# Gated linear attention with a two-way maxout layer: another order of the first loads, another split of one weight difference, and other costs in the planner

## The chip, the cores and the metric

The kernel runs on one core of one Trainium2 chip. The metric is the device time of one execution in microseconds (us); lower is better. One core has TensorE (PE in the profile, its weight loads PEld), VectorE (DVE), ScalarE (ACT), GpSimd (POOL) and SyncE (SP), which here issues every DMA.

## The reference

Inputs are q, k, v and alpha of shape (4, 8, 768, 48): 4 batch elements, 8 heads, 768 tokens, 48 values per head. For each batch element and head a 48x48 state runs over the tokens, and its output rows become the tokens of a two-way maxout layer with weights w1, w2 (384x1024) and w_out (1024x384). The output is (3072, 384) in float32.

```python
for t in range(S):
    state = alpha[:, :, t, :, None] * state + np.einsum('bhd,bhe->bhde', k[:, :, t], v[:, :, t])
    y[:, :, t] = np.einsum('bhd,bhde->bhe', q[:, :, t], state)
x = np.ascontiguousarray(y.transpose(0, 2, 1, 3)).reshape(B * S, H * D)
out = np.maximum(x @ w1, x @ w2) @ w_out
```

## The kernel before

**The attention half.** The 768 tokens of the first batch element are taken as three "doubles" of 256 tokens (written (0, h), (1, h), (2, h), with h = 0, 1 for the two halves of the heads); the other 2304 tokens as 18 "singles" of 128 tokens, numbered 6 to 23. Each goes through the same steps: the logarithm of alpha on ACT (`a1`); sums over the tokens on PE (`p1`, tile dcs or cs); the two exponentials `en` and `ep` and the small `gg` on ACT; k times `en` on POOL (`kt`); q times `ep` on DVE (`qt`); eight transposes on PE (`p2`, tile dtp or tp) and one copy of them (`v2`, tile dqk or qk, on ACT or DVE); the products of q and k on PE (`p3`, tiles dpa and dpb, in a ring of two PSUM buffers); two masked copies of these on DVE (`m0`, `m1`, tile dpt or pt); the state's update (`pk` or `kv` on PE, `w` on DVE, tile dw, and `g`, `t32`, `T0`, `T1` on POOL); the output y on PE (`p4`, tile dy or y); and its copy into xT on ACT (`a3`).

**The maxout half.** Since max(a, b) = b + relu(a - b), the kernel forms wd = w1 - w2 (`prep_wd`, tile wd16: six pieces of 128x512, four on DVE and two on POOL) and m = w2 @ w_out (`w2c` converts w2, `w2t` transposes it on PE, `w2te` copies the transposes, `m` multiplies by the converted w_out `wo16`, `mev` copies the result). The tokens that are in xT are taken in groups of one to three blocks of 128. For each group there are eight steps `f` (three matmuls h = wd x, then a relu on ACT or DVE into g16), and for each block two steps `t`: half 0 (three matmuls with m, three with w_out) and half 1 (five with w_out). `oev` copies the finished block and `st` stores it. The tiles h, op, mp and y share a ring of three PSUM buffers.

**What sets the order.** A planner, class Sched, runs while the kernel is built. Each step is an Op with a cost per engine, the steps that it depends on (`deps`, which count in the planner's clock), steps that only have to be placed before it (`after`), the buffers that it allocates and reads, and a priority. Whenever an engine is free by the planner's clock, the ready step with the earliest start is placed next in that engine's queue. On the chip each engine runs its queue in that order and waits at a step whose inputs are not there. `refill` forms the groups of the maxout half when PE would have nothing else to do. So a cost that is changed moves nothing by itself, but may change the order of all queues.

**The loads.** SP issues them in one queue: the first double in seven DMAs, w2 in one, w_out in two halves, w1 in two halves (columns 0 to 511 and 512 to 1023), the second and third doubles in four DMAs of 384 KB each (alpha, k, q, v), then the singles, which reuse the memory of the weights. The first four of the eight `f` steps of a group need the first half of wd, the others the second:

```python
            o = op("f", a, {"PE": 3 * max(W / 2400 + 0.0025, 0.07)}, lambda e, a0=a0, W=W, f=f: fstep(a0, W, f),
                   lat=0.17, deps=xs + wdc[f // NFH], after=pend[-1:], alloc=[bh] + ([bg] if f == 0 else []), prio=1000 + a)
```

Of the kernel before, what the change touches and what calls it, by code (L numbers as in the profile page):

```python
# [49 lines left out]
class Sched:  # L50
# [49 lines left out]
    def run(self):  # L100
        while True:
            c = self.pick("PE")
            if c and self.refill:
                self.refill(c[1], c[1] > self.free["PE"] + 0.3)
            best = None
            for e in self.todo:
                c = self.pick(e)
                if c and (best is None or c[1] < best[0]):
                    best = (c[1], e, c[2])
            if best is None:  # L110
                if self.refill and self.refill(1e9, True):
                    continue
                break
            t, e, op = best
            cost = op.engs[e]
            if e == "PE" and op.tiled != self.tiled:
                cost += 0.09
                self.tiled = op.tiled
            if e == "SP":
                t = max(t, self.wire - 4.0)  # L120
                self.wire = max(self.wire, t + 0.7) + cost
                op.done = self.wire + op.lat
                cost = 0.45
            else:
                op.done = t + cost + op.lat
            self.free[e] = t + cost
            for b in op.alloc:
                b.ring.taken.append(b)
            for x in op.engs:
                self.todo[x].remove(op)  # L130
            op.fn(e)
        assert not any(self.todo.values()), {e: [(o.name, o.n) for o in v][:5] for e, v in self.todo.items()}
# [3 lines left out]
def kernel(  # L136
# [21 lines left out]
    nc = tc.nc  # L158
# [485 lines left out]

    def prep_wd(e, s, i):
        c = slice(i * FH, (i + 1) * FH)
        eng = nc.vector if e == "DVE" else nc.gpsimd
        eng.tensor_sub(out=wd16[:, s, c], in0=w1f[:, s, c], in1=w2f[:, s, c])  # L648

# [68 lines left out]
    def op(*a, **k):  # L718
        return Op(S, *a, **k)
# [31 lines left out]

    dloads_of(0, 0.0)
    lw2 = prev = op("w2", 0, {"SP": WLOAD}, lambda e: load_w2(), lat=1.6, after=[prev], prio=0.5)
    lw1, lwo = [], []
    for kind in ("wo", "w1"):
        for i in range(2):
            fn = {"wo": load_wo, "w1": load_w1}[kind]
            prev = op(kind, i, {"SP": WLOAD / 2}, lambda e, i=i, fn=fn: fn(i), lat=1.6, after=[prev], prio=0.5)
            (lwo if kind == "wo" else lw1).append(prev)
    dloads_of(1, 0.3)  # L760
    dloads_of(2, 0.6)

    w2c = [
        op("w2c", s, c, lambda e, s=s: copy(e, w216[:, s, :], w2f[:, s, :]), deps=[lw2], prio=0.6)
        for s, c in enumerate(({"ACT": 0.95}, {"DVE": 0.65}, {"ACT": 0.95, "DVE": 0.65}))
    ]
    wdc = [[op("wd", s, {"POOL": 1.2} if s == 2 else {"DVE": 0.68}, lambda e, s=s, i=i: prep_wd(e, s, i),
               deps=[lw1[i], lw2], prio=0.6) for s in range(3)] for i in range(2)]
    woc = [op("woc", f, {"ACT": 0.75, "DVE": 0.55},
# [26 lines left out]
    sp1 = op("pads", 1, {"DVE": 0.5}, lambda e: set_pads(1), prio=0.9)  # L796
    smask = op("mask", 0, {"DVE": 1.0}, lambda e: set_mask(), prio=0.1)
    sdv = [op("dvT", i, {"POOL": 0.6}, lambda e, i=i: set_dvT(i), prio=(-1, 0.9)[i]) for i in range(2)]
    sone = [op("one", i, {"POOL": 0.8}, lambda e, i=i: set_single(i), prio=1.5) for i in range(4)]


    rdloga, rdqt, rdkt, rdv, rdT, rdw, rdt32, rdgg, rdg = (Ring(2) for _ in range(9))
    B2 = []
    for m in range(ND):
# [11 lines left out]
        def add(name, h, engs, fn, deps, lat=0.1, alloc=(), reads=(), **kw):  # L816
            o = GD[m - 1].get((name, h)) if m else None
            g[name, h] = op("d" + name, (m, h), engs, fn, lat=lat, deps=deps, after=[o, g.get((name, h - 1))],
                            alloc=[B[x] for x in alloc], reads=[B[x] if not isinstance(x, Buf) else x for x in reads],
                            prio=2 * m + 0.3 * h, **kw)  # L820
            return g[name, h]

        for h in range(2):
            al = lambda x: [x] if h == 0 else []
            re = lambda x: [x] if h else []
            add("a1", h, {"ACT": 0.43}, lambda e, m=m, h=h: d1(m, h), [g["ld", 0, h], sp1 if m == 1 else None],
                alloc=al("loga"), reads=[L[0]] + re("loga"))
            add("p1", h, {"PE": 0.5}, lambda e, m=m, h=h: dcs(m, h), [g["a1", h]], lat=0.17, alloc=[("cs", h)], reads=["loga"])
            add("en", h, {"ACT": 0.39}, lambda e, m=m, h=h: dexp(m, h, "en", -1.0), [g["p1", h]],
                alloc=al("en"), reads=[("cs", h)] + re("en"))  # L830
            add("ep", h, {"ACT": 0.39}, lambda e, m=m, h=h: dexp(m, h, "ep", 1.0), [g["en", h]],
                alloc=al("ep"), reads=[("cs", h)] + re("ep"))
            add("gg", h, {"ACT": 0.2}, lambda e, m=m, h=h: dgg(m, h), [g["ep", h]],
                alloc=al("gg"), reads=[("cs", h)] + re("gg"))
            add("kt", h, {"POOL": 1.0}, lambda e, m=m, h=h: dqk(m, h, 1), [g["en", h], g["ld", 1, h]],
                alloc=al("kt"), reads=["en", L[1]] + re("kt"))
            add("qt", h, {"DVE": 0.7}, lambda e, m=m, h=h: dqk(m, h, 2), [g["ep", h], g["ld", 2, h]],
                alloc=al("qt"), reads=["ep", L[2]] + re("qt"))
# [3 lines left out]
                alloc=[("tp", h)], reads=["qt", "kt"])  # L842
            add("v2", h, {"DVE": 0.64, "ACT": 0.92}, lambda e, m=m, h=h: dtpe(e, m, h), [g["p2", h]],
                alloc=[("qk", h)], reads=[("tp", h)])
            add("p3", h, {"PE": 0.36}, lambda e, m=m, h=h: dp(m, h), [g["v2", h]], lat=0.17,
                alloc=[("pa", h), ("pb", h)], reads=[("qk", h)], tiled=True)
            for t in range(2):
                add("m" + str(t), h, {"DVE": 0.62}, lambda e, m=m, h=h, t=t: dmask(m, h, t),
                    [g["p3", h], smask, g.get(("m0", h))],
                    alloc=[] if t else [("pt", h)], reads=[(("pa", "pb")[t], h)] + ([("pt", h)] if t else []))  # L850
# [27 lines left out]
    for n in range(2 * ND, NCG):  # L878
# [8 lines left out]
        def add(name, engs, fn, deps, lat=0.1, alloc=(), reads=(), **kw):  # L887

            g[name] = op(name, n, engs, fn, lat=lat, deps=deps, after=[dep(n - 1, name) if name != "a3" or n > 2 * ND else None],
                         alloc=[B[x] for x in alloc], reads=[B[x] if isinstance(x, str) else x for x in reads],  # L890
                         prio=n, **kw)
            return g[name]
# [3 lines left out]
        add("en", {"ACT": 0.39}, lambda e, n=n: a2(n, "en", -1.0), [g["p1"]], alloc=["en"], reads=["cs"])  # L896
        add("ep", {"ACT": 0.39}, lambda e, n=n: a2(n, "ep", 1.0), [g["en"]], alloc=["ep"], reads=["cs"])
        add("gg", {"ACT": 0.2}, lambda e, n=n: a2g(n), [g["ep"]], alloc=["gg"], reads=["cs"])
        add("kt", {"POOL": 1.0}, lambda e, n=n: v1k(n), [g["en"], g["ld", 1]], alloc=["kt"], reads=["en", L[1]])
# [99 lines left out]
```

## Time and profile before

| | |
|---|---|
| median of 8 runs | 152.04 us (151.12 to 153.51) |
| profiled execution, its time | 152.05 us |
| its span in the profile | 150.2 us |
| PE busy | 133.9 us (89%) |
| DVE, ACT, POOL busy | 89.2, 97.6, 89.7 us |
| longest shares of the chain that ended last | PE 75%, DMA 9%, DVE 6% |
| bytes moved | 28.65 MB, mean 191 GB/s |

The page of the profile gives the busy time of each engine and the chain of work that ended last, followed back from the last instruction. Other views show instructions in order of time (start, duration, engine, line, operation, what it writes and reads, how often, and in brackets how long the engine had been idle and what ended that), or busy times by stretches of the span. Several instructions of one kind that follow each other are put on one line. The profiled execution's time stands 1.85 us above its span and within 0.01 us of the median.

### The profile page before, as it was taken

The page shows a single profiled execution, that of the slowest core. Times are in us where ns is not written, and L with a number is a line of the kernel's source. Part 1 is how long each engine was busy: PE and PEld are TensorE (multiplying, and loading weights), DVE is VectorE, ACT ScalarE, POOL GpSimd, SP SyncE. Part 2 cuts the span into 40 slices and gives each one's busy share as a digit, 9 for nine tenths or more (in the row PEclk, how much of TensorE's full clock was granted, in tenths as well). Part 3 has the DMA queues.
Part 4 walks back from the last instruction along what each step waited for, and adds up shares of the span by engine and source line. Part 5 has one row for each costly group of instructions (what it writes and reads, how often), then busy time and mean ns, then how long its engine had stood idle before and what let it go on. Part 6 is the DMA issues. An engine that isn't in the chain of part 4 may idle for free.

```text
span 150.2 us, 5349 instructions
## 1 busy us (share of the span) xinstructions
PE 133.9 (89%) x2198; PEld 90.3 (60%) x2198; DVE 89.2 (59%) x168; ACT 97.6 (65%) x217; POOL 89.7 (60%) x184
## 2 busy tenths in 40 slices
PE   0464895996899999999999999999999999999990
PEld 0443864775787666666656666666576665666550
DVE  4776578669694987748574898659688750000000
ACT  4446753757775996879649984698747953845721
POOL 7998043869976788975775978549696920000000
PEclk9999999999699999999999999999999999999999
DMA  4999999999988897989889999898979502103112
GB/s 121 277 397 368 381 317 219 273 246 193 254 172 162 164 228 149 199 195 210 186 176 204 246 226 200 168 236 198 223 152 241 167 4 105 52 4 118 39 68 89
DMA packets 92888, 28.65 MB, mean 191 GB/s; under 512 B 87872, under 2 KB 91968, under 8 KB 92736
## 3 DMA queue, kind: packets, MB, share of 16 engines
q1 hardware_dynamic: 92864, 28.32, 79.0%
q8 instruction: 17, 0.28, 0.7%
q14 instruction: 7, 0.06, 0.1%
HBM read 23.59 MB, written 4.72 MB: 188 GB/s over the span
## 4 chain that ended last, share of the span: by engine, by line
PE 75%; DMA 9%; DVE 6%; SPq 4%; ACT 2%; issue 2%; POOL 0%; ACTq 0%; POOLq 0%
PE h L679 21%; PE op L696 21%; DMA w1f<-in_moe_w_dram 9%; PE op L693 8%; PE y L449 4%; PE pa L401 4%; DVE wd L648 3%; PE tp L383 3%; PE y L443 3%; PE tp L385 3%; SPq L201 2%; PE cs L324 2%; PE kv L412 2%; PE dy L613 2%; PE dtp L520 1%
## 5 line engine op out<-in xcount | busy, mean ns | idle before, releaser
L679 PE MATMUL h<-xT,wd 128*128 128x384 f16 (+2 forms) x216 | 37.4, 312 | 1.6 <-DVE m L643 1.6
L696 PE MATMUL op<-wo,g 128*128 128x384 f16 x192 | 37.3, 326 | 0.0
L686 ACT ACTIVATE g<-h 128x384 f16<-128x384 f32 (+2 forms) x54 | 24.3, 463 | 2.7 <-PE h L679 2.2
L679 PEld LDWEIGHTS <-wd 128*128 128x128 f16 x216 | 18.8, 100 | 11.0 <-issue 1.8
L696 PEld LDWEIGHTS <-g 128*128 128x128 f16 x192 | 17.8, 97 | 11.2
L420 DVE TENSOR_TENSOR pt<-pa,u 128x512 f16<-128x512 f32 x18 | 12.4, 689 | 9.2 <-PE pb L401 6.7
L643 ACT COPY outs<-op 128x384 f32<-128x384 f32 x17 | 8.1, 479 | 14.5 <-PE op L696 14.5
L643 ACT COPY qk<-tp 128x1024 f16<-128x1024 f16 x14 | 14.2, 1015 | 2.9 <-PE tp L385 2.7
L362 POOL TENSOR_TENSOR T<-w,g 48x192 f16<-48x192 f32 x30 | 15.2, 508 | 1.1
L693 PE MATMUL op<-m,xT 128*128 128x384 f16 x72 | 15.6, 326 | 0.1
L456 ACT CAST xT<-y 128x384 f16<-128x384 f32 x18 | 8.7, 485 | 6.8 <-PE y L449 6.8
L420 DVE TENSOR_TENSOR pt<-pb,u 128x512 f16<-128x512 f32 x18 | 12.3, 682 | 0.1
L684 DVE TENSOR_SCALAR g<-h 128x384 f16<-128x384 f32 (+2 forms) x18 | 8.9, 503 | 4.6 <-PE h L679 4.3
L449 PE MATMUL y<-pt,v 128*32 128x128 f16 x432 | 11.0, 219 | 0.0
L431 DVE TENSOR_TENSOR w<-kv,t 48x192 f32<-48x192 f32 x24 | 8.5, 354 | 4.2 <-PE kv L412 3.2
L334 ACT ACTIVATE en<-cs 128x384 f32<-128x384 f32 x18 | 8.9, 494 | 1.7 <-PE cs L328 1.7
L334 ACT ACTIVATE ep<-cs 128x384 f32<-128x384 f32 x18 | 9.0, 498 | 0.0
L449 PEld LDWEIGHTS <-v 128*32 128x32 f16 x432 | 8.4, 97 | 0.7 <-issue 0.6
L370 POOL TENSOR_TENSOR t<-w,g 128x192 f32<-128x192 f32 x12 | 7.7, 638 | 2.0 <-DVE w L429 1.7
L693 PEld LDWEIGHTS <-xT 128*128 128x128 f16 x72 | 6.5, 98 | 3.9 <-issue 0.3
L346 POOL TENSOR_TENSOR kt<-wof,en 128x384 f16<-128x384 f32 x6 | 6.0, 997 | 4.7 <-DMA wof<-in_v_dram 2.4
L443 PE MATMUL y<-qk,T 112*32 112x128 f16 x180 | 8.7, 223 | 0.0
(122 smaller groups left out, 281.4 us busy)
## 6 DMA issues: line engine op xcount, KB each, us to landing
out_dram<-outs SPq DMA_DIRECT2D x24, 192.0 KB, 2.7
w2f<-in_moe_w_dram SPq DMA_DIRECT2D x1, 1536.0 KB, 9.0
wof<-in_moe_w_out_dram SPq DMA_DIRECT2D x2, 768.0 KB, 10.6
w1f<-in_moe_w_dram SPq DMA_DIRECT2D x2, 768.0 KB, 12.4
dvf<-in_v_dram SPq DMA_DIRECT2D x3, 384.0 KB, 5.7
wof<-in_alpha_dram SPq DMA_DIRECT2D x6, 192.0 KB, 3.9
wof<-in_k_dram SPq DMA_DIRECT2D x6, 192.0 KB, 4.0
wof<-in_q_dram SPq DMA_DIRECT2D x6, 192.0 KB, 4.2
```

The source lines that it names most:

```text
L334: nc.scalar.activation(out=t, in_=csv, func=ACTF.Exp, scale=scale)
L362: nc.gpsimd.tensor_mul(out=st[n]["T16"][ps, :, :, 16 * t : 16 * t + 16], in0=st[n - 1]["w"][ps].rearrange("p (r s) e -> p r s e", s=3), in ...
L420: nc.vector.tensor_mul(out=s["pt"][:, t], in0=s["pp"][t], in1=ub)
L443: nc.tensor.matmul(y[32 * r : 32 * r + 32, i, :], lhsT=T16[0:112, r, i, :], rhs=s["qk"][0:112, r, :], start=True, stop=False,)
L449: nc.tensor.matmul(y[32 * r : 32 * r + 32, i, :], lhsT=v16[:, r, i, 16 * t : 16 * t + 32], rhs=s["pt"][:, t, r, :], start=(first and t == ...
L456: nc.scalar.copy(out=xT[:, :, n * C : (n + 1) * C], in_=st[n]["y"])
L643: {"ACT": nc.scalar.copy, "DVE": nc.vector.tensor_copy, "POOL": nc.gpsimd.tensor_copy}[e](out=out, in_=in_)
L679: nc.tensor.matmul(h[:, 0:W], lhsT=wd16[:, s, f * 128 : (f + 1) * 128], rhs=xT[:, s, a : a + W], start=(s == 0), stop=(s == 2))
L684: nc.vector.tensor_relu(gts[a][:, f, 0:W], hs[a, f][:, 0:W])
L686: nc.scalar.activation(out=gts[a][:, f, 0:W], in_=hs[a, f][:, 0:W], func=ACTF.Relu)
L693: nc.tensor.matmul(op, lhsT=xT[:, s, t0 : t0 + C], rhs=m16[:, s, :], start=(s == 0), stop=False)
L696: nc.tensor.matmul(op, lhsT=gts[a][:, f, i * C : (i + 1) * C], rhs=wo16[:, f, :], start=False, stop=(f == NF - 1))
```

## The change

The change has five parts.

1. The four DMAs of the second double are issued between w_out and w1, and no longer behind w1.
2. wd is formed by two DVE instructions of 128x3x512 (one for each half of w1), and no longer by four on DVE and two on POOL of 128x512.
3. In the planner `ep` and `gg` depend on `p1` and have only to be placed behind `en` and `ep` of the same half. Before, they depended on `en` and `ep`.
4. Costs in the planner are changed: all PE steps before 19.0 us of its clock count 1.9 times, the mask's set-up 1.5 for 1.0, and those of the doubles' steps rise by a few hundredths to 0.2.
5. Through these the planner makes other queues. Of what the order of instructions shows: on PE, y of the first double (dy) stands behind three of the four groups of transposes of w2 instead of ahead of them; the sums, transposes and products of the second double stand between the matmuls of m instead of behind them and behind the first three `f` steps; y of the second double stands ahead of half 1 of the first `t` step. On DVE the two wd instructions stand ahead of the second double's masks (dpt) and updates (dw). The maxout groups have 2, 1, 3, 3, 3, 3, 3, 3, 3 blocks before, and 2, 3, 3, 3, 3, 3, 3, 3, 1 after.

```diff
@@ Sched.run
             cost = op.engs[e]
+            if e == "PE" and t < 19.0:
+                cost *= 1.9
@@
-    def prep_wd(e, s, i):
+    def prep_wd(i):
         c = slice(i * FH, (i + 1) * FH)
-        eng = nc.vector if e == "DVE" else nc.gpsimd
-        eng.tensor_sub(out=wd16[:, s, c], in0=w1f[:, s, c], in1=w2f[:, s, c])
+        nc.vector.tensor_sub(out=wd16[:, :, c], in0=w1f[:, :, c], in1=w2f[:, :, c])
@@
-    dloads_of(0, 0.0)
-    lw2 = prev = op("w2", 0, {"SP": WLOAD}, lambda e: load_w2(), lat=1.6, after=[prev], prio=0.5)
-    lw1, lwo = [], []
-    for kind in ("wo", "w1"):
-        for i in range(2):
-            fn = {"wo": load_wo, "w1": load_w1}[kind]
-            prev = op(kind, i, {"SP": WLOAD / 2}, lambda e, i=i, fn=fn: fn(i), lat=1.6, after=[prev], prio=0.5)
-            (lwo if kind == "wo" else lw1).append(prev)
-    dloads_of(1, 0.3)
-    dloads_of(2, 0.6)
+    lw1, lwo = [None] * 2, [None] * 2
+    for x in "d0 w2 wo0 wo1 d1 w10 w11 d2".split():
...
-    wdc = [[op("wd", s, {"POOL": 1.2} if s == 2 else {"DVE": 0.68}, lambda e, s=s, i=i: prep_wd(e, s, i),
-               deps=[lw1[i], lw2], prio=0.6) for s in range(3)] for i in range(2)]
+    wdc = [[op("wd", i, {"DVE": 1.7}, lambda e, i=i: prep_wd(i), deps=[lw1[i], lw2], prio=0.6)] for i in range(2)]
@@
-    smask = op("mask", 0, {"DVE": 1.0}, lambda e: set_mask(), prio=0.1)
+    smask = op("mask", 0, {"DVE": 1.5}, lambda e: set_mask(), prio=0.1)
+    AFTER = {"ep": "en", "gg": "ep"}
@@ the doubles
-            g[name, h] = op("d" + name, (m, h), engs, fn, lat=lat, deps=deps, after=[o, g.get((name, h - 1))],
+            g[name, h] = op("d" + name, (m, h), engs, fn, lat=lat, deps=deps, after=[o, g.get((name, h - 1)), g.get((AFTER.get(name), h))],
@@
-            add("ep", h, {"ACT": 0.39}, lambda e, m=m, h=h: dexp(m, h, "ep", 1.0), [g["en", h]],
+            add("ep", h, {"ACT": 0.44}, lambda e, m=m, h=h: dexp(m, h, "ep", 1.0), [g["p1", h]],
@@
-            add("gg", h, {"ACT": 0.2}, lambda e, m=m, h=h: dgg(m, h), [g["ep", h]],
+            add("gg", h, {"ACT": 0.2}, lambda e, m=m, h=h: dgg(m, h), [g["p1", h]],
@@
-            add("qt", h, {"DVE": 0.7}, lambda e, m=m, h=h: dqk(m, h, 2), [g["ep", h], g["ld", 2, h]],
+            add("qt", h, {"DVE": 0.9}, lambda e, m=m, h=h: dqk(m, h, 2), [g["ep", h], g["ld", 2, h]],
```

The singles' `ep` and `gg` are changed in the same way, and the other costs of the doubles (`a1` 0.43 to 0.45, `en` 0.39 to 0.44, `kt` 1.0 to 1.05, `v2` 0.64 and 0.92 to 0.66 and 0.95, `m0` and `m1` 0.62 to 0.66) likewise.

## The prediction

> **What bounds the kernel now.** I read the page first. PE is busy for 89% of the span, its bar is full from the twelfth slice on, and PE holds 75% of the chain that ended last.
>
> ```profile
> PE 133.9 (89%) x2198; PEld 90.3 (60%) x2198; DVE 89.2 (59%) x168; ACT 97.6 (65%) x217; POOL 89.7 (60%) x184
> PE   0464895996899999999999999999999999999990
> PE 75%; DMA 9%; DVE 6%; SPq 4%; ACT 2%; issue 2%; POOL 0%; ACTq 0%; POOLq 0%
> ```
>
> Next, the busy times by stretches (first the stretch, its length and PE's busy time; then PEld, DVE, ACT, POOL, granted clock, DMA share, GB/s).
>
> ```profile
> 0.00:10.00 10.00, 3.34 (x40) 2.66 (x40) 5.78 (x21) 4.92 (x10) 8.70 (x36) 1.00 0.84 245
> 10.00:20.00 10.00, 7.23 (x194) 5.79 (x195) 6.59 (x13) 6.32 (x8) 4.39 (x13) 1.00 1.03 381
> 20.00:30.00 10.00, 8.34 (x75) 6.07 (x74) 7.93 (x10) 5.21 (x15) 6.09 (x5) 1.00 1.12 257
> 30.00:40.00 10.00, 8.27 (x256) 6.20 (x253) 7.71 (x12) 6.36 (x15) 8.63 (x17) 0.93 1.10 227
> 40.00:60.00 20.00, 20.00 (x416) 14.29 (x412) 15.43 (x31) 15.47 (x38) 15.81 (x31) 0.95 0.89 181
> 60.00:100.00 40.00, 40.00 (x696) 26.34 (x683) 27.58 (x51) 29.77 (x67) 28.37 (x54) 1.00 0.96 204
> ```
>
> All of PE's idle time lies in the first 40 us: 40 - 27.2 = 12.8. From 40.1, where PE starts the last transposes of the third double, to its end at 146.7, it never stops. The amount of PE work is the same in both kernels, so the end is set by how much of it is done when PE becomes continuously busy. What matters is the first 40 us, and the last group.
>
> Third, the instructions in order of time, 20 to 26 and 34 to 39 us.
>
> ```profile
> 20.32 4.64 DVE L648 TENSOR_TENSOR wd<-w1f,w2f 128x512 f16<-128x512 f32 x4 [0.39 <-DMA w1f<-in_moe_w_dram]
> 20.42 1.72 POOL L648 TENSOR_TENSOR wd<-w1f,w2f 128x512 f16<-128x512 f32 x1 [5.95 <-issue]
> 22.45 1.35 POOL L648 TENSOR_TENSOR wd<-w1f,w2f 128x512 f16<-128x512 f32 x1 [0.32 <-DMA w1f<-in_moe_w_dram]
> 24.88 0.55 DVE L643 CAST m<-mp 128x384 f16<-128x384 f32 x1
> 34.80 0.99 POOL L508 TENSOR_TENSOR dkt<-dkf,den 128x384 f16<-128x384 f32 x1
> 35.13 1.08 DVE L506 TENSOR_TENSOR dqt<-dqf,dep 128x384 f16<-128x384 f32 x1
> 38.42 1.17 PE L613 MATMUL dy<-dpt,dv 64*32 64x128 f16 x76 [0.57 <-DVE dpt L548]
> ```
>
> Here the limit is DVE. Four wd pieces take 4.64; the fastest takes 0.68, so four alone would be near 2.5. DVE stands still while POOL computes its own wd pieces. The same shows at 35.13: dqt takes 0.55 where it runs alone and 1.08 behind POOL's dkt, ending 0.42 after it. PE waits for such DVE steps: 1.59 before 25.48 for the cast of m, 0.57 before 38.42 for a mask.
>
> **Part 1, the loads.** In the DMA views w1's halves land at 20.3 and 22.4 (issue plus time to landing), the second double's four at 23.7, 25.1, 26.5 and 27.9, the third double's alpha at 29.4, w_out's second half at 17.7. Landings follow the order of issue and the channel never rests (DMA share 0.9 to 1.25), so I swap the blocks: the double needs 27.9 - 22.4 = 5.5 and lands at 19.1, 20.5, 21.9 and 23.3, 4.6 earlier. w1's first half needs the 2.55 of before and lands at 25.85, its second at 27.9: 5.5 later. The third double does not move. No store is queued on SP there, so SP's waits delay nobody.
>
> What fills PE meanwhile: transposes of w2 from about 15.7 (the second conversion of w2 ends at 15.65), y of the first double (1.86, as at 14.52), then the second double. Its logarithms end near 20.2 (alpha 19.1, ACT 0.52 each), its sums at 20.9, the last transposes of w2 and their copy at 21.9. From there: m, six of 0.65; the double's transposes 0.9; its first products 0.33; its state matmuls 0.37: 27.4. Before wd PE has nothing more.
>
> **Part 2, wd.** Two DVE instructions of 1536 columns. No row shows this size. Lower bound: three pieces at the 0.60 from start to start that they take alone, 1.8. Upper bound: three at the 1.68 that pieces behind POOL took, 5.0. From dqt (384 columns, 0.55) to the piece (512, 0.68) it is 0.13 per 128 columns, so 0.55 + 9 x 0.13 = 1.75. I take this, nearest the lower end, because POOL has no wd of its own now; it still has small operations of 0.5 to 0.7 for the second double, of which half of one (0.35) stands before the first instruction and less (0.15) before the second.
>
> **Part 3, the wait that is added.** On DVE the two instructions stand ahead of the second double's masks. So DVE waits for w1, and behind it wait the cast of m, masks, updates and relus, and for these PE, whose two product buffers come free only with the masks. Starts, from rows of before:
>
> - wd's first half 25.9; done 25.9 + 0.35 + 1.75 = 28.0 (PE's first `f` step follows); cast of m 0.47: 28.5; second half, landed by then, 1.9: 30.4.
> - masks 0.60 + 0.60 with a state update 0.27 between: 31.9; two relus of 0.35 and the other update 0.27: 32.8; the next mask 0.60: 33.4; the third double's dqt 0.95 (behind POOL, as at 35.13): 34.4.
> - PE: its transposes 0.45: 34.9; half 0 of the first `t` 0.97, y of the second double 1.38, products 0.33, state matmuls 0.37, transposes 0.45, sums of single 6 0.33: 38.7; half 1 of the first `t` 0.81: 39.5; its result comes 0.17 later and is copied out on DVE in 0.56, with two hand-overs of 0.05 to 0.1, before the buffer is free: the second `t` step starts at 40.4.
>
> **What that start is worth.** Before, from 40.1 to 146.7 there are 106.6 left. Of these 0.86 are a half clock: transposes 0.83 for 0.45, three `f` steps 0.97 for 0.49. At the second `t` step the changed queue has this step's 1.88 (1.07 + 0.81) still to do, and has done transposes 0.45, state matmuls 0.37 and products 0.27 that before had not: 0.79 more. Add the tail, 0.8, below: 107.3. For an unchanged end the second `t` step would have to start at 146.7 - 107.3 = 39.4. It starts at 40.4: a loss of 1.0.
>
> **Part 4, the tail.** The last group has one block for three. A step `f` then takes 0.165 on PE (42.67: 128 columns) and its relu 0.28. With three buffers PE waits 0.4 for the copy of block 22 (0.17 + 0.48 + hand-overs, less two `f` steps) and twice 0.2 for relus: 0.8. Before, a step takes 0.49 there against a relu of 0.38 from start to start, and PE waits for nothing.
>
> **Part 5, what costs nothing.** The exponentials by halves: ACT runs them back to back either way (26.41 to 28.2); dqt gets `ep` 0.4 earlier, POOL's second dkt its `en` 0.5 later, hidden behind POOL's first dkt (0.99). If POOL were idle there, it would cost that 0.5. The planner's new costs act only through the queues above.
>
> **The clock.** The granted clock, in stretches of 3.4 us:
>
> ```profile
> 21.70:25.10 3.40, 2.19 (x16) 1.38 (x15) 3.40 (x4) 1.69 (x4) 1.79 (x2) 1.00 1.02 224
> 35.40:38.80 3.40, 1.96 (x97) 1.60 (x103) 3.03 (x5) 2.61 (x7) 3.26 (x6) 0.96 0.97 214
> 38.80:42.20 3.40, 3.40 (x103) 2.83 (x85) 2.58 (x4) 2.04 (x6) 3.24 (x6) 0.53 1.09 243
> ```
>
> After a stretch with PE busy for 1.96 the clock was halved for the next 3.4; after one with 2.19 it was not. In the changed kernel PE has 1.85 of work between 28.0 and 31.9, where the first masks end (three `f` steps at 0.33, two sums at 0.43). If the clock is halved behind it, up to 1.1 of the work between 32 and 35.4 comes on top, less what hides behind the DVE queue.
>
> The Trainium skill (TensorE: Matmul & The Clock Gate, Part 1: The HAM clock gate) says that half rate follows an idle window of about 3.4 us. Read as a wholly idle one, it would leave this 1.1 out, but it would not allow the drop at 38.8 either, so the row decides.
>
> **The rivals.**
>
> A, the forecast: DVE's queue behind w1 and the tail: 152.05 (the profiled execution's own time; the median is 152.04) + 1.0 = 153.0. Against it: POOL, and so DVE, has less to do than before. Own range 152.3 to 153.6, by wd's waits for POOL and the landing (0.4). Chance 0.40.
>
> B, the same and a half clock that shows: + 1.1 = 154.1; or wd twice at up to 3, same size. For it: 1.85 is less than 1.96. Against it: the stretches need not fall like this, and until 34.4 DVE is the limit. Chance 0.27.
>
> C, no change: the queue holds, but the port is free more often: no waits for POOL (0.5) and w1 0.45 earlier, as halves of 2.1 would give: 152.1. For it: DVE's small waits at 35.13 come from dkt alone. Against it: POOL's queue is full there (8.63 of 10 us). Chance 0.17.
>
> D, faster: POOL's work is the mechanism. Its two wd pieces (3.07) are gone and the second double's k is multiplied 5 earlier, so POOL is through before DVE needs the port. Place: DVE's queue from 25.9 to 34.4. Price: wd's waits 0.5, dqt 0.4, w1 0.45 and one relu on ACT instead 0.35 to 0.7: together 1.8, 151.2. It decides if the second `t` step starts before 38.6. Against it: DVE's wait for w1 stays, and so does the tail. Chance 0.16.
>
> That the change doesn't do what it says is excluded by the order of instructions, save that the loads might share the channel instead of queueing; w1 would land earlier, as in C.
>
> **How the numbers follow.** A measurement of this kernel can tell about 0.5%, 0.76 us, from no change. Slower than 152.8: 0.29 of A's 0.40 and all of B, 0.56. Within: the other 0.11 of A, C, and 0.01 of D, 0.29. Faster: the rest of D, 0.15. The range reaches past D's 151.2 and B's 154.1, to 151.0 and 154.7; some 0.2 for D and B beyond these are left out.
>
> **What would show it.** Right: a DVE wait for DMA w1f of 2 us or so near 24 to 26, wd twice at 1.75 to 2.1, PE gaps between 27.6 and 32.2 released by wd, the cast of m, and masks, a second `t` step at 40.4, some 0.8 of PE gaps before the last op. Wrong: w1 landed well before 25, wd above 3 or PE's last gap before 38.6.

## The result, and the profile after

The changed kernel takes 155.33 us (median of 11 runs, 153.46 to 156.44) against 152.33 for the kernel before on the same chip: ratio 1.0166, 95% interval 1.0129 to 1.0203. A second set of runs gave 1.0118 (1.0067 to 1.0168). So it is slower by 1.2 to 1.7%, 1.8 to 2.5 us, where +1.0 was forecast; the range ended at 154.7. (Ratios compare undisturbed runs only, so they need not be the quotient of the medians.)

The page of the profile after; its profiled execution took 155.34, its span is 153.6:

```profile
PE 135.2 (88%) x2198; PEld 90.1 (59%) x2198; DVE 87.3 (57%) x162; ACT 100.0 (65%) x221; POOL 88.7 (58%) x182
PE   0453969779998999999999999999999999999990
PEclk9999999987999999999999999999999999999998
...
q8 instruction: 17, 0.28, 0.8%
...
PE 76%; DMA 14%; SPq 4%; ACT 3%; issue 1%; ACTq 0%
PE h L680 22%; PE op L697 21%; PE op L694 8%; DMA wof<-in_moe_w_out_dram 7%; DMA daf<-in_alpha_dram 6%; PE y L451 4%; PE pa L403 4%; PE tp L385 3%; PE y L445 3%; PE tp L387 3%; SPq L203 2%; PE cs L326 2%; PE kv L414 2%; PE dy L615 2%; SPq L222 1%
```

PE's bar is full from the fourteenth slice on, before from the twelfth. DVE, 6% of the chain before, is gone from it, and so is w1. DMA has gone from 9% to 14%: 7% are w_out, and 6% are daf, the alpha of the third double, a load that the prediction had said would not move.

Busy times by stretches (columns as before: PE, PEld, DVE, ACT, POOL, clock, DMA share, GB/s):

```profile
0.00:10.00 10.00, 3.11 (x41) 2.80 (x42) 4.94 (x20) 4.54 (x9) 8.70 (x40) 1.00 0.85 241
10.00:20.00 10.00, 6.48 (x190) 5.26 (x183) 7.58 (x12) 5.83 (x9) 4.73 (x9) 1.00 1.09 336
20.00:30.00 10.00, 8.48 (x116) 5.21 (x116) 5.18 (x6) 5.79 (x13) 7.15 (x9) 1.00 1.00 287
30.00:40.00 10.00, 8.20 (x206) 6.23 (x207) 7.02 (x11) 6.80 (x18) 7.05 (x12) 0.83 0.83 181
```

The last column is the one to compare. Before: 245, 381, 257 and 227, together 11.10 MB in the first 40 us; after: 10.45, and 10.84 when the same kernel was profiled again. At 181 to 227 GB/s the 0.26 to 0.65 MB that are missing are 1.1 to 3.6 us of the load stream. PE is busy for 8.20 from 30 to 40, as before (8.27), but 3.4 us of this stretch lie at half clock (1.4 before).

The instructions in order of time; the lines that answer to the forecast:

```profile
21.57 0.24 PE L478 MATMUL dcs<-dloga,c 128*128 128x192 f16 x1 [1.10 <-issue]
...
26.70 2.14 DVE L649 TENSOR_TENSOR wd<-w1f,w2f 128x1536 f16<-128x1536 f32 x1 [1.30 <-DMA w1f<-in_moe_w_dram]
27.18 2.02 POOL L601 TENSOR_TENSOR dT<-dw,dg 48x192 f16<-48x192 f32 x1
29.95 1.76 DVE L649 TENSOR_TENSOR wd<-w1f,w2f 128x1536 f16<-128x1536 f32 x1 [0.64 <-DMA w1f<-in_moe_w_dram]
31.23 0.52 ACT L467 ACTIVATE dloga<-daf 128x384 f16<-128x384 f32 x1 [4.11 <-DMA daf<-in_alpha_dram]
31.62 0.68 DVE L550 TENSOR_TENSOR dpt<-dpa,cmask 128x512 f16<-128x512 f32 x1
31.80 0.24 PE L477 MATMUL dcs<-dloga,c 128*128 128x192 f16 x1 [1.96 <-ACT dloga L467]
33.79 3.16 PE L680 MATMUL h<-xT,wd 128*128 128x256 f16 x15
36.79 0.39 PE L522 MATMUL dtp<-ident,dqt 128*128 128x128 f16 x4
47.24 0.23 PE L615 MATMUL dy<-dpt,dv 64*32 64x128 f16 x1 [0.69 <-issue]
```

DVE stands behind w1 as forecast, but it waits twice where one wait was forecast, and its first mask starts at 31.62 against 30.4. PE's longest wait behind 20 us ends with alpha, by ACT, not with a mask: between 20 and 50 us PE has no wait over 0.25 for DVE; the fifteen f matmuls take 3.0 instead of 1.65 at half clock; and two waits have no releaser but "issue".

### The profile page after: what moved, and what is told of

Same layout as the page of the kernel before. It is cut to its first block, busy times and chain, and to the rows that moved or that the text cites. A ratio compares the mean times of both kernels' runs of the same rounds, so it can differ in the third digit from the quotient of the medians.

```text
span 153.6 us, 5348 instructions
## 1 busy us (share of the span) xinstructions
PE 135.2 (88%) x2198; PEld 90.1 (59%) x2198; DVE 87.3 (57%) x162; ACT 100.0 (65%) x221; POOL 88.7 (58%) x182
## 4 chain that ended last, share of the span: by engine, by line
PE 76%; DMA 14%; SPq 4%; ACT 3%; issue 1%; ACTq 0%
PE h L680 22%; PE op L697 21%; PE op L694 8%; DMA wof<-in_moe_w_out_dram 7%; DMA daf<-in_alpha_dram 6%; PE y L451 4%; PE pa L403 4%; PE tp L385 3%; PE y L445 3%; PE tp L387 3%; SPq L203 2%; PE cs L326 2%; PE kv L414 2%; PE dy L615 2%; SPq L222 1%
## 5 line engine op out<-in xcount | busy, mean ns | idle before, releaser
L645 ACT COPY outs<-op 128x384 f32<-128x384 f32 x19 | 9.1, 481 | 16.5 <-PE op L697 16.5
L694 PE MATMUL op<-m,xT 128*128 128x384 f16 x72 | 15.6, 326 | 0.0
L645 ACT COPY qk<-tp 128x1024 f16<-128x1024 f16 x13 | 13.2, 1012 | 2.3 <-PE tp L387 2.1
L510 POOL TENSOR_TENSOR dkt<-dkf,den 128x384 f16<-128x384 f32 x6 | 6.2, 1046 | 7.5 <-ACT den L492 7.4
L348 POOL TENSOR_TENSOR kt<-w2f,en 128x384 f16<-128x384 f32 x6 | 6.0, 1000 | 7.6 <-issue 3.3
L477 PE MATMUL dcs<-dloga,c 128*128 128x192 f16 x6 | 1.6, 270 | 8.3 <-ACT dloga L467 8.3
```

Source lines behind the costliest of these rows:

```text
L348: nc.gpsimd.tensor_mul(out=kts[n % NB][:, :, 0:D], in0=loads[n][1], in1=st[n]["en"])
L645: {"ACT": nc.scalar.copy, "DVE": nc.vector.tensor_copy, "POOL": nc.gpsimd.tensor_copy}[e](out=out, in_=in_)
L694: nc.tensor.matmul(op, lhsT=xT[:, s, t0 : t0 + C], rhs=m16[:, s, :], start=(s == 0), stop=False)
```

## The experiments

### The three parts, each alone and two by two

Six kernels separate the parts: the order of loads, the two large wd, and the costs with the orders of exponentials. Each edit moves one part, and the planner then makes a new queue for it:

```diff
 # loads: before                        after
-"d0 w2 wo0 wo1 w10 w11 d1 d2"
+"d0 w2 wo0 wo1 d1 w10 w11 d2"
 # wd
-eng.tensor_sub(out=wd16[:, s, c], in0=w1f[:, s, c], in1=w2f[:, s, c])   # s = 0, 1 DVE, 2 POOL
+nc.vector.tensor_sub(out=wd16[:, :, c], in0=w1f[:, :, c], in1=w2f[:, :, c])
 # costs
+if e == "PE" and t < 19.0: cost *= 1.9      # with ep and gg on p1, mask 1.5 and the small ones
```

**b_loads_only**: the kernel before with the new order of loads.

> The kernel before with the second double's four loads ahead of w1, nothing else; the planner arranges the queues anew with its old costs. If the place of w1 is the cause (theory 1), w1's halves land near 26.7 and 29.9 as in the changed kernel, and the time rises by 1.5 to 3 us, to 153.6 to 155. If the form of wd (theory 2) or the planner's new costs (theory 3) are the cause, it stays within 0.8 us of before.

**b_wd_only**: the kernel before with the two large wd.

> The kernel before with wd by two DVE instructions of 128x1536, nothing else. Theory 1 expects no loss: DVE's 4.64 us for four pieces become 3.5 to 4.0 for two, and PE's wait of 1.59 us for the cast of m shrinks by as much, so 151.3 to 152.3. Theory 2 (long DVE instructions hold what is queued behind them and shut POOL out) expects 153 or more. Theory 3 expects no difference.

**b_costs_only**: the kernel before with the new costs and orders.

> The kernel before with the planner's new costs and dependences alone; loads and wd as before. If the place of w1 alone makes the loss (theory 1), ratio 0.99 to 1.005. If the queues that the costs make are a cause by themselves (theory 3), 1.008 to 1.02.

**a_costs_back**: new loads and wd, old costs.

> The changed kernel with the planner's costs and the exponentials' dependences of before; loads and wd as changed. Theory 1 expects that it stays slow, 154 to 156, with a DVE wait of over 1 us for w1 near 25. Theory 3 (the queues that the new costs make) expects 152.8 or less.

**a_loads_back**: new wd and costs, old loads.

> The changed kernel with the old order of loads (w1's halves before the second double); the two large DVE subtractions and the new costs, orders of exponentials and so the planner's new queues stay. Theory 1 (the price is what lands late: w1 by 6, and behind it the third double by 1 to 2): w1 lands near 20.8 and 23.0, the masks of the second double no longer wait for it, PE has at most 1 us of gaps between 25 and 40, and the time is 152 to 152.8, as before the change. Theory 2 (the price is in the planner's queues, which the new costs set): the time is that of the costs alone with the old subtractions, 156.5 to 158, with PE's gaps near the transposes of w2 (22.4: 1.66 there) and in y of the third double (48.2: 1.22 there); the form of the subtraction moves it by less than 0.5.

**a_wd_back**: new loads and costs, old wd.

> The changed kernel with the old subtraction (four pieces on DVE, two on POOL); new loads and new costs stay. Theory 1 (the two large instructions cost nothing by themselves, as they did alone: 1.0005): 153.8 to 155.5, 1.012 to 1.022 of before, with w1 at 26 to 28 and 29 to 30.5. Rival (two large instructions on DVE are what puts the masks behind w1's second half): 152.0 to 153.3, and the first mask of the second double starts before 30. If it is slower than 155.5, the two large instructions were a gain in this queue, by POOL's time.

The changed kernel was run again beside them (**after_again**):

> The changed kernel once more, on the chip of the next three runs. If the half clock (33.2 to 36.6 in its first profile) is part of the price and not chance, it is there again, within 2 us; PE's wait inside the first sums of the second double (1.1 us at 21.6, released by nothing that the profile shows) and inside y of the third double (0.7 us at 47.2) are there again if they hang on the program and not on chance. Ratio 1.015 to 1.02.

| loads | wd | costs | ratio to before | 95% interval |
|---|---|---|---|---|
| new | old | old | 1.0135 | 1.0041 to 1.0228 |
| old | new | old | 1.0005 | 0.9954 to 1.0056 |
| old | old | new | 1.0356 | 1.0304 to 1.0408 |
| new | new | old | 1.0041 | 0.9981 to 1.0100 |
| old | new | new | 1.0263 | 1.0211 to 1.0315 |
| new | old | new | 1.0210 | 1.0179 to 1.0241 |
| new | new | new | 1.0166, 1.0118 | 1.0129 to 1.0203, 1.0067 to 1.0168 |

The parts do not add up. Of the theories in these expectations, theory 1 (the place of w1) holds in b_loads_only and a_wd_back, but a_costs_back has new loads and no loss clear of noise, and a_loads_back has old loads and 1.0263. b_costs_only came dearer than either of its theories had it, after_again (1.0118) below its 1.015. The two large wd cost nothing alone. The costs, which the prediction put at nothing beyond the order that it had read, are the dearest part, and dearest where the loads stay as they were. With all three parts the kernel is faster than with the costs alone: the new order of loads and the large wd give back half or more of what the new costs take. A row is not the price of one part by itself, since every kernel has a queue of its own: with the new costs and the old loads the planner forms ten groups (1, 1, 3, 3, 3, 3, 3, 3, 3, 1) and PE has 2222 matmuls instead of 2198.

### Is it the wait for w1?

**a_wd_no_w1** has the queues of the changed kernel, but w1's part is left out:

```diff
-in0=w1f[:, :, c], in1=w2f[:, :, c]
+in0=w2f[:, :, c], in1=w2f[:, :, c]
```

> The changed kernel with the same queues and loads, but wd is formed from w2 alone (w2 - w2), so DVE does not wait for w1; w1 is still loaded. If DVE's wait for w1 sets the start of what follows (theory 1), the two wd end near 27.5 and 29.8 instead of 28.8 and 31.7, the masks come 1.9 us earlier, and the time falls by 1 to 2 us, to 153.5 to 154.5. If the third double's later alpha (landing 31.1 where 29.4 was) sets it, through PE's queue, the time falls by less than 0.4.

Measured: 1.0133 (1.0033 to 1.0232). With the wait that the forecast rested on gone, the loss is still there, though with three runs in the ratio a return of 1 us is neither shown nor excluded. PE waits 1.30 for the third double's alpha (landed 31.61) and, for no releaser, 1.74 at 22.4 and 1.16 at 46.9.

### Is it the half clock?

**a_pe_kept_busy** has 32 matmuls that are thrown away, ahead of the third double's sums:

```diff
+for _ in range(32 if (m, h) == (2, 0) else 0):
+    nc.tensor.matmul(cs[:, 0:128], lhsT=c11, rhs=ident16, start=True, stop=True)
```

> The changed kernel with 32 more matmuls of 128x128 on PE ahead of the third double's first sums, into a buffer that these sums then overwrite; nothing else moves. They fill the 2 us in which PE waits for the third double's alpha. If the half clock behind this wait costs what its longer matmuls show (theory 4: 3.0 us for five f steps that take 1.65 at full clock), the half clock is gone and the time falls by 1.0 to 1.5 us against the changed kernel. If DVE's queue is the limit there anyway (theory 1), the clock stays full and the time falls by less than 0.4.

Measured: 1.0210 (1.0162 to 1.0258), and the half clock behind the wait is gone. But the profiled execution does not settle the question, since its clock became full only at 27.6, in the profile above at 19.5:

```profile
26.07 0.63 PE L524 MATMUL dtp<-ident,dqt 128*128 128x128 f16 x4
27.89 0.39 PE L524 MATMUL dtp<-ident,dqt 128*128 128x128 f16 x4
```

The half clock lies elsewhere in other executions: at 33.2 to 36.6 in the profile above, at 22.9 to 26.3 when the same kernel was profiled again. In a_wd_no_w1 (above) and a_shift100 (below) the clock is full from 20.9 and 20.4 to the end of PE's work, and the loss is there. So half clock makes one execution differ from the next, but does not explain the loss.

### Is it the tail?

**a_groups_213** forms a group of one block as the second and leaves none for the end:

```diff
-while k < WMAX // C and a + k ...
+lim = 1 if a == 2 else WMAX // C
+while k < lim and a + k ...
```

> The changed kernel with the second group of the maxout half held to one block, so that the groups are 2, 1, 3, 3 and so on as before and the last has three blocks; up to there the queues are the same. If the last group of one block costs the 0.8 us of the prediction, the time falls by 0.5 to 1.0 us; if it costs nothing, or the early single block costs the same, by less than 0.3.

Measured: 1.0141 (1.0076 to 1.0206), no gain that can be told apart. In the profile of the changed kernel PE waits 0.28 at 146.7 and nowhere else behind 50.

### The waits that nothing releases

Queue q8 of the page holds the clue: 17 packets, 0.28 MB. That is 16 KB a packet for 2198 matmuls with as many weight loads, so near 64 bytes an instruction and 128 matmuls a packet; the kernels below with 2294 and 2298 matmuls have 18 packets. Numbering PE's matmuls from 0, the two waits of the changed kernel are at 223 and 735, which are 4 x 128 apart. In all 20 profiles there are 32 waits of more than 0.25 us within one of matmul 95 + 128 k that end 2.2 to 3.2 us after the start of a packet of q8 (31 of them 2.2 to 2.75; b_loads_only alone has none); no border is passed sooner than 2.18 after its packet starts, and where PE came to one later than that, it did not wait for this. PE waits there for its own instructions.

The trace of before showed one as well:

```profile
18.89 0.45 PE L654 MATMUL wtp<-ident,w 128*128 128x128 f16 x5 [0.48 <-issue]
```

It is the same border, 223. In the changed kernel the packet started at 18.82 instead of 16.32, since PE passed the border ahead of it (95) at 15.9 instead of 12.7: the first double's second copy dqk, which ACT made before, is made by DVE with the new costs, at 14.85 and behind a conversion of w2, and PE's wait for it grew from 0.54 to 2.69. With the old costs (a_costs_back) both borders are back at 12.7 and 18.9.

**a_code_shift** tests it: 64 small matmuls, thrown away, in an idle time near 7 us move every later instruction by half a packet.

```diff
+for _ in range(64 if (m, h) == (0, 1) else 0):
+    nc.tensor.matmul(cs[:, 0:16], lhsT=c11, rhs=ident16[:, 0:16], start=True, stop=True)
```

> The changed kernel with 64 matmuls of 16 columns ahead of the first double's second sums (near 7 us, where PE waits 1.98 for the logarithms): work that is thrown away, in time that was idle. It moves every later instruction of PE by 64 matmuls, half of what one 16-KB packet of PE's instruction queue holds (2198 matmuls with as many weight loads in 17 packets: near 129 matmuls each). Theory (PE's two waits that nothing releases, 1.10 at 21.6 and 0.69 in y of the third double, are waits for its own instructions): they leave the places they have had in every run of this program: the one at 21.6 moves 64 matmuls earlier, into the transposes or y of the first double, the one in y to another part of it or away; the time moves by up to 1.5 either way, 153.3 to 155.5. Rival (they belong to the work there: a semaphore or memory port that the profile misses): both stay where they were, 0.7 to 1.4 each, and the time is 153.8 to 155.3.

Measured: 1.0173 (1.0124 to 1.0221). Both waits are gone from their places; a new one stands in the third double's state matmuls, at matmul 607 = 223 + 3 x 128:

```profile
42.49 0.36 PE L569 MATMUL dkv<-dv,dkt 64*64 64x48 f16 x11 [1.04 <-issue]
```

That PE waits for its own instructions is shown; the time did not move. So the next kernels moved the borders to where PE is slower, by 72 or 100 small matmuls at the same place, and took the other late things away with them.

**a_shift100** (n = 100 in the changed kernel):

```diff
+for _ in range(n if (m, h) == (0, 1) else 0):
+    nc.tensor.matmul(cs[0:32, 0:16], lhsT=ident16[:, 0:32], rhs=c11[:, 0:16], start=True, stop=True)
```

> The changed kernel with 100 small matmuls of 16 columns ahead of the first double's second sums, thrown away, near 7 us where PE waits for 1.98. In every run so far PE's waits without a releaser stand at matmul 95 + 128 k (223, 607, 735), 2.3 to 2.75 us after the start of a 16-KB packet of the instruction queue, and only where PE ran through 128 matmuls too soon for it. This shift puts these borders where the trace of the changed kernel has 5.4, 11.2, 4.4, 5.9 and 3.6 us between them (without the shift 5.7, 11.2, 6.4, 5.4 and 2.7 with the waits in them). Theory (instruction fetch is part of the loss and stands on its own): the waits at 21.6 and in y of the third double are gone, at most 0.3 comes in their place, and the time falls by 0.7 to 1.8 against the changed kernel, to 152.8 to 154.3. Rival (the late w1 and the late third double stand behind the first wait in any case, so only the second, 0.7 to 1.2, comes back or nothing does): 154.3 to 155.5, with PE waiting longer before its first f steps and before the third double's sums.

**a_no_w1_shift100** (with wd = w2 - w2 as well):

> The same 100 matmuls in the kernel whose wd is w2 - w2 (w1's part is left out, so nothing waits for w1). That kernel without them: 154.35, with waits of 1.74 and 1.16 at the borders and 1.30 for the third double's alpha. Theory (w1's landing and the instruction fetch cover each other: each alone gives back little, both together most of the loss): 151.8 to 153.3, 0.998 to 1.008 of before. Rival (the rest of the loss lies in the queues and in the third double's late loads): 153.3 to 154.8.

**a_w1_third** (wd = w2 - w2, a third of w1 loaded, no shift):

```diff
-out=w1f[:, :, c], in_=...[:, :, c]
+out=w1f[:, 0:1, c], in_=...[:, 0:1, c]
```

> The changed kernel with wd = w2 - w2 and only one of w1's three row blocks loaded (256 of 768 KB in each half; two thirds of w1 and its part in wd are left out): every load behind w1 lands some 2.5 to 3 earlier, the third double's alpha near 28 instead of 30.3 to 31.6, and the borders of the instruction queue stay where they were. Theory (what is left of the loss is the load stream, which runs late behind w1 for the third double and the first singles): 152.0 to 153.4, with the wait for alpha near 31 gone and the two waits at the borders still there (1.1 to 1.7 at 21.6, 0.7 to 1.2 in y of the third double). Rival (the queues of the new costs): 153.6 to 155.

**a_w1_third_shift100**:

> The same with the 100 small matmuls that take PE's waits at the borders away: no wait for w1, an earlier load stream, no waits for instructions. Theory: all of the loss and more is given back, 150.3 to 152.3, 0.990 to 1.003 of before. Rival (queues): 153 or more; PE then waits in the second double and third double for DVE, ACT or POOL, not for a DMA or its own instructions.

| kernel | w1's wait | waits at borders, us | third double's alpha lands | ratio | 95% interval |
|---|---|---|---|---|---|
| changed | there | 1.8, 2.7 | 31.1, 30.3 | 1.0166, 1.0118 | 1.0129 to 1.0203, 1.0067 to 1.0168 |
| a_wd_no_w1 | gone | 2.9 | 31.6 | 1.0133 | 1.0033 to 1.0232 |
| a_shift100 | there | 0.3 | 30.3 | 1.0200 | 1.0149 to 1.0250 |
| a_no_w1_shift100 | gone | 1.0 | 30.5 | 1.0167 | 1.0115 to 1.0220 |
| a_w1_third | gone | 3.1 | 27.0 | 1.0097 | 1.0063 to 1.0131 |
| a_w1_third_shift100 | gone | 1.2 | 26.9 | 1.0034 | 1.0002 to 1.0066 |

In a_shift100 and a_no_w1_shift100 the theory's time failed, and the rival's came: fewer border waits gave nothing back. a_w1_third came where its theory had it, a_w1_third_shift100 just above.

Two of PE's waits in a_no_w1_shift100 (who waited, for whom, us in total, times, longest):

```profile
PE cs L326 <- ACT loga L321: 1.3, 1, 1.3
PE h L682 <- ACT gg L340: 1.0, 1, 1.0
```

and in order of time what ACT waited for ahead of the first of them, and the weight loads beside the second:

```profile
42.41 0.52 ACT L321 ACTIVATE loga<-wof 128x384 f16<-128x384 f32 x1 [1.42 <-DMA wof<-in_alpha_dram]
...
48.67 0.42 PEld L682 LDWEIGHTS <-wd 128*128 128x128 f16 x3 [1.20 <-issue]
```

The first is a single's alpha: with w1's wait and most of the border waits gone, PE runs into the load stream. The second is put down to ACT's gg, which h does not read. It is matmul 862, the weight loads beside it wait for "issue", and it ends 2.56 after a packet's start: a border that the shift has not cleared. The same stands in the other two shifted kernels of the table (0.32 and 1.16).

Why the first border wait gave nothing back stands in the traces. When the changed kernel was profiled again, and in a_wd_no_w1, the third double's alpha and its first sums read:

```profile
30.41 0.52 ACT L467 ACTIVATE dloga<-daf 128x384 f16<-128x384 f32 x1 [2.00 <-DMA daf<-in_alpha_dram]
30.99 0.24 PE L477 MATMUL dcs<-dloga,c 128*128 128x192 f16 x1
31.70 0.52 ACT L467 ACTIVATE dloga<-daf 128x384 f16<-128x384 f32 x1 [3.77 <-DMA daf<-in_alpha_dram]
32.27 0.24 PE L477 MATMUL dcs<-dloga,c 128*128 128x192 f16 x1 [1.30 <-ACT dloga L467]
```

In seven of the eleven profiles with this queue (the changed kernel's two, a_wd_no_w1, a_groups_213, a_code_shift, a_shift100, a_no_w1_shift100) these sums start 0.66 to 0.67 after alpha lands, at 30.3 to 31.6. In the five of them with full clock from there on, the second `t` step starts 9.2 to 9.4 later, and PE waits for nothing over 0.25 in between. So it starts at 40.19 with DVE's wait for w1 and at 41.48 without it (a_wd_no_w1): alpha sets it, not w1. With alpha at 27 PE comes to these sums only at 30.0 (a_w1_third), or 29.3 with the shift, so the late alpha holds them back by 1.0 to 2.3 us.

Only where the stream is earlier (alpha at 27 instead of 30 to 31.6) do fewer border waits pay: 1.0097 becomes 1.0034 (the intervals meet only at their ends), and most of the loss is given back. What makes the loss is therefore, as far as shown, the late alpha of the third double with the border waits beside and behind it; w1's own landing lies hidden behind alpha. Which share belongs to which can't be given, because each hides the others. One reservation: the last two kernels also load 1 MB less than any full version must, and the kernel before was not run with as little, so it is not excluded that part of what came back is the smaller load alone.

**b_costs_shift72** asks how much of the dear costs is instruction fetch, with n = 72 in b_costs_only, which waits 1.66, 0.34 and 1.22 at borders:

> The kernel before with only the new costs and orders (157.69 by itself, 1.0356, with waits at the borders of 1.66 at 22.4, 0.34 at 43.6 and 1.22 at 48.2, 3.2 in all), with 72 small matmuls near 7 us: between the borders lie then 10.8, 10.3, 6.9, 4.6 and 5.0 us. Theory (what the planner's new queues cost with the old loads is for the most part instruction fetch, since they put the dense y of the doubles close behind a border): the three waits are gone and the time falls by 2.2 to 3.4, to 154.3 to 155.5. Rival (the waits are one face of a queue that is late anyway): it falls by less than 1.5, to 156.2 or more.

Measured: 1.0276 (1.0230 to 1.0321) instead of 1.0356: 1.2 us back by the ratios, which is the rival's, 1.8 by the medians (155.87 for 157.69), which lies between the two; the intervals still touch. The three waits are gone from their places. PE's waits now, the first of them hidden before:

```profile
PE h L683 <- DVE wd L652: 1.4, 1, 1.4
...
PE y L451 <- DVE w L433: 0.8, 1, 0.8
```

The second is a border again (matmul 863, 2.26 after a packet's start; that y does not read w), so 2.4 of the 3.2 were taken away and half or more of them came back as time. By these middle values a fifth to a third of what the costs take alone is instruction fetch, which the touching intervals do not settle; the rest, the order of the queues with what it hides, is not taken apart further.

**b_shift20** was meant to beat both, with n = 20 in the kernel before and its wait of 0.48 in view:

> The kernel before with 20 small matmuls near 6.6 us, where PE waits 1.75. Its border at matmul 223 costs 0.48 at 18.9; shifted by 20 it has at least 4.6 us between any two borders. Theory: this wait is gone, and since PE is not yet continuously busy there and waits 1.59 for the cast of m later, no more than 0.4 comes back: 151.6 to 152.2, 0.997 to 1.001. Rival (a shift costs by itself, in the time of the matmuls or by a later border): 152.5 or more.

Measured: 1.0049 (1.0016 to 1.0083), slower; the expectation fell. The wait at border 223 did not vanish but grew to 1.16, inside y of the first double, though the borders were 6 us apart: the packet started only at 15.23, PE was at the border 1.2 later and went on 2.35 after its start. Distance between borders is not the rule; the time from the packet's start is. Why a packet starts when it does, from 3.4 us ahead of the border before to 5.3 behind it, stays open.

### Why the load stream is late

The order of loads alone loses it: b_loads_only, same view as above.

```profile
10.00:20.00 10.00, 7.70 (x194) 6.08 (x194) 6.44 (x13) 6.39 (x8) 4.37 (x13) 1.00 0.97 308
20.00:30.00 10.00, 6.38 (x101) 4.11 (x99) 4.50 (x6) 5.01 (x13) 5.75 (x7) 0.97 1.00 295
30.00:40.00 10.00, 9.32 (x153) 6.18 (x154) 8.48 (x13) 5.76 (x16) 8.13 (x11) 0.69 0.95 202
```

With 248 in the first stretch that is 10.53 MB by 40 us; the costs alone keep 10.94. In the changed kernel SP is held by the issue of the second double's loads (10.75, 14.41, 17.87), so w1's halves are issued at 19.28 and 20.71, where before they were issued at 7.3 and 10.7 and waited in the channel.

**a_w1_act** lets ACT issue w1:

```diff
-nc.sync.dma_start(out=w1f[:, :, c], ...)
+nc.scalar.dma_start(out=w1f[:, :, c], ...)
```

> The changed kernel with w1's two halves issued by ACT, between its copies of w_out and of w2's transposes, instead of by SP behind the second double's last load. Theory (w1 was late since SP issued it only at 19.3 and 20.7, held by the issue of small packets): w1 lands by 25.0 and 27.5, the second double 1 to 2 later than 23.6, and the masks' wait is gone, 152.8 to 153.8. Rival (the channel's bytes set the landing, whoever issues): w1's second half lands at 28.5 or later, the second double's v at 24 to 26, and the time stays at 153.8 to 155.5.

Measured: 1.0329 (1.0297 to 1.0360), the slowest with the new loads. w1 landed at 23.69 and 26.36, 3.0 and 3.6 earlier, and 10.91 MB were moved by 40 us, so w1 was late because SP issued it late. But the second double's q and v then shared the channel and landed at 26.99 and 28.27 instead of 22.34 and 23.57, and PE waited 2.27 for them at 27.7; half clock, at 22.2 to 25.6 and 29.1 to 32.5, came on top in this execution. Neither expected time came. The channel gives one what it takes from the other.

## Why the prediction was wrong

The direction was right, and in part the place: a slower kernel, for the most part by what happens in the first 40 us. The size was not: +3.0 in the first set of runs, +1.7 in the second, against +1.0 (by the medians). The step that failed is the path: the forecast let DVE's queue behind w1 set the second `t` step, held the third double still, and had no term for PE's waits for its own instructions. The runs show in its place that the third double's alpha, landing at 30.3 to 31.6 instead of 29.4, sets that step, with or without DVE's wait for w1, and that PE waits 0.69 to 1.21 for instructions behind it.

- **The balance at the second t step** holds. From its start to PE's end the forecast had 107.3 with a tail of 0.8, so 106.5 without. The profile above: 42.34 to 149.99 is 107.65, less 0.69 (border) and 0.28 (tail): 106.68. The same kernel profiled again: 40.19 to 148.37, less 1.21 and 0.28: 106.69. What failed is the start and what was left out behind it. Against the forecast's end (40.4 + 107.3 = 147.7) the start gives +1.94 in the first execution and -0.21 in the second, the border wait +0.69 and +1.21, the tail -0.52, the rest +0.19: 2.3 and 0.7 on top of the forecast's 1.0, as PE's ends show (149.99 and 148.37, before 146.68). That 40.19 lies so near 40.4 is luck, since alpha led there and not the masks.
- **Part 1, the loads** is where the failure began. The second double landed as forecast (19.6 to 23.6 against 19.1 to 23.3), but w1 at 26.68 and 29.93 against 25.85 and 27.9, in other runs with this order 26.2 to 28.8 and 28.9 to 30.8. "The third double does not move" was wrong by 0.9 to 2.6 (alpha 30.3 to 32.0 against 29.4). The swap of blocks of landing times took for granted that w1, queued later, would move as fast as before.
- **"Before wd PE has nothing more" from 27.4**: m ended at 28.9, 1.5 later. Missing was the wait of 1.10 for instructions. It stood in the trace of before as 0.48 <-issue and in the page as 2% issue, and had no term.
- **Part 2, wd** was right: 1.76 alone and 2.14 beside POOL's operations, so 0.38 more, against 1.75 (its sum comes to 1.72) and 0.15 to 0.35 more.
- **Part 3, DVE's queue** ran near its times, but PE did not wait for it: dqt(2, 0) ended at 35.16 against 34.4, 0.76 late, no more than w1's first landing (0.83). Behind it the transposes started 1.63 later still, since the f steps ahead of them ran at half clock: rival B's mechanism, in this execution (10.54 from the third double's sums to the second `t` step, 9.2 at full clock).
- **Part 4, the tail** was over-sized: 0.28 against 0.8.
- **Part 5, "costs nothing"** was wrong. The order of the new queues was read rightly, but PE's wait of 2.69 at 15.6 was passed over since PE was idle in the first 20 us anyway. It moved PE's instruction packets and through them the border at 21.6. The costs alone, with the old loads and wd, took 1.0356.
- **The clock** came as the row had it, not as the wholly idle window would: half clock followed a stretch of 3.4 us in which PE had been idle for 1.96. It changes place between executions of one kernel.
- **The rivals**: C and D are out. B came nearest in size, for a reason that explains one execution and not the loss: with the clock full from 20.9 and 20.4 on (a_wd_no_w1, a_shift100) the loss is there too.

One step of the reasoning failed as well: taking one wait, making it the limit, and pricing the change by it. Here three late things lay within 2 us of each other.

## What to carry to other kernels

Ahead of a change to a start-up phase, list every stream that ends within a few us of the one in view, the engine's own instructions and the later loads among them: the wait that is removed or added is worth only the distance to the next one. Read "issue" waits as a term with a price: number the matmuls, see whether the waits repeat at a fixed distance, and ask whether the change brings dense small matmuls closer to such a border. A planner's costs are part of a change like any other; a queue that is ready "in an idle time anyway" can still move what comes behind it.

## What the runs showed of the hardware

- At every 128th matmul PE can wait for its own instructions, here 0.3 to 1.8 us: it went on 2.2 to 2.75 us (once 3.2) after the start of a 16-KB packet of the instruction queue, which itself took 0.88 to 1.7.
- While the first wd instruction ran (26.70 to 28.84) POOL's operation dT took 2.02; the next of the same form took 0.50. The Trainium skill (SBUF - State Buffer, SBUF: two separate sides) states that of a DVE operation with two SBUF inputs and a GpSimd operation that reads SBUF, the one that starts first holds the pair of ports that they share for the whole instruction. The rows agree: dT ended 0.36 after wd.
- The clock column begins with its first record, at 17.5 to 27.6 us in the 20 profiles. Ahead of it the column says 1.00, but PE ran at half clock: four transposes took 0.61 at 10.23 in the trace of before and 0.39 at 29.54.
- Behind that, in stretches of 3.4 us cut at the clock's own changes, half clock followed twelve times in the first 60 us of the 20 profiles, each time after a stretch with PE busy for 0.97 to 1.84 us; after every stretch there with more the clock stayed full. Near the end, among wide matmuls, it stayed full after 1.46 to 1.78 too, so busy time alone is not the rule. So a border wait can bring half clock with it: when the changed kernel was profiled again, the wait of 1.44 at 21.6 left PE busy for 1.70 of the 3.4 us from 19.5 on, and 22.9 to 26.3 ran at half clock.
- Half clock lay at 38.6 to 42.0, 33.2 to 36.6, 22.9 to 26.3, or nowhere before the end, in executions of kernels that are nearly the same. The Trainium skill (TensorE: Matmul & The Clock Gate, Part 1: The HAM clock gate) calls its window free-running; stretches of 3.4 us that begin at another time in each execution agree with that.
